# A new order for the head of a diffusion-transformer block: batch 0's roots on ScalarE, both of batch 0's K steps first, 2-byte statistics outputs

## The chip, the cores and the metric

One core of one Trainium2 chip. The metric is the device time of one execution in microseconds (us), as the median of several; executions of the kernel before spread from 243.1 to 244.75 us over all runs. "The profile" is one traced execution; its times count from the start of the span. PE is TensorE (PEld its weight loads), DVE VectorE, ACT ScalarE, POOL GpSimd, SP the engine that issues the loads.

## The reference, cut to what matters

```python
B, N, D = 2, 256, 1152            # bf16; F = 4 * D
mod = (_silu(c) @ w_mod).reshape(B, 6, 1, D)
shift_a, scale_a, gate_a, shift_m, scale_m, gate_m = [mod[:, i] for i in range(6)]
h = _layernorm(x, axis=-1) * (1 + scale_a) + shift_a
qkv = (h @ wqkv).reshape(B, N, 3, H, Dh)
...  # attention, wo, a second layernorm, fc1, gelu, fc2
```

The change touches only the way from `x` and `c` to the first matmuls of `K = h @ wk`. The 512 tokens lie in four tiles of 128: tiles 0 and 1 are batch 0, tiles 2 and 3 are batch 1. D is cut into 9 chunks of 128. The shift is added later; K needs `layernorm(x) * (1 + scale_a)`, transposed.

## The kernel before: the parts that matter

Statistics of tiles 1 and 3 are made on VectorE (`bn_stats`), those of tiles 0 and 2 on ScalarE, by two passes over 1152 elements whose outputs nobody reads; only the accumulated sums count.

```python
for t in (0, 1, 3, 2):                                   # order in which x lands
    nc.sync.dma_start(x_sb[:, t, :], x_v[:, t // TPB, t % TPB, :])
# then scale weights of chunks 0-1, K weights of 0 and 1, scale of 2-3, K of 2-3, scale of 4-5, ...
...
sink = act.tile([P, D], FP32, name="sink", tag="x1")
def act_stats(t):
    for f, dst in ((ACT.Identity, dsum), (ACT.Square, dsq)):
        nc.scalar.activation(sink[:], x_sb[:, t, :], f, bias=x_sb[:, t, 0:1], scale=-1.0,
                             accum_out=dst[:, t:t + 1])
def norm1(t, c0, c1):                                    # VectorE: (x - mean) * rstd
    ...
def scale_group(k0, k1, tile_of=aux_tile):               # PE: scale of chunks k0..k1 into pm
    ...
def modulate(pt, i, k, b, j0, eng):                      # hT0[k] of batch b = transposed xn * scale
    ...
def k_step(k, c0=0, c1=T, m0=0, m1=KM1):                 # chunk k of six K accumulators, tokens c0..c1
    for m in range(m0, m1):
        if k == 0 and c0 == 0:
            pk[m] = acc_tile([P, T], "pk")
        nc.tensor.matmul(pk[m][:, c0:c1], w_k[:, k, m * P:(m + 1) * P], hT0[:, k, c0:c1], ...)
...
warm(8, pwarm)                                           # matmuls on zeros while data comes
act_stats(0)
act_stats(2)
...
pool_rsqrt(0, 2)                                         # GpSimd: roots of tiles 0 and 1
...
norm1(1, 0, CUT)
norm1(0, 0, CUT)
pt_a = transpose_x([0, 1], BT[0])
...
pm0, pm1 = [scale_group(k, k + 1, acc_tile) for k in range(2)]
act_var(2)
nc.vector.tensor_scalar_mul(hT0[:, 0, 0:N], pt_a[:, 0, :], pm0[:, 0, 0:1])
...
transpose_x([0, 1], [3], pt_c, 1)
fill(1)                                                  # one more matmul on zeros
k_step(0, 0, N)                                          # batch 0, chunk 0
transpose_x([0, 1], [2], pt_c, 0)
k_step(1, 0, N)                                          # batch 0, chunk 1
modulate(pt_c, 0, 0, 1, 0, "d")
modulate(pt_c, 1, 1, 1, 0, "a")
...
k_step(0, N, T)                                          # batch 1, chunk 0
```

Every engine here runs its own instructions in program order (in c_before below VectorE idles 0.88 us in front of a variance, while batch 0's modulation stands behind it). "K step (k, b)" below is the six matmuls of chunk k for batch b.

## Time and profile before

243.88 us, median of 3 (243.38 to 244.41).

The page's busy time of PE, and the shares of the chain of waits:

```profile
PE 236.1 (98%) x1691; PEld 145.0 (60%) x1701; DVE 91.4 (38%) x193; ACT 59.8 (25%) x120; POOL 28.9 (12%) x48
...
PE 91%; DMA 3%; DVE 3%; ACT 1%; issue 1%; SPq 0%; POOL 0%; DVEq 0%; ACTq 0%
```

PE is the limit, so a change of the head can win only by letting PE's useful work begin earlier, or by closing gaps there. The timeline of PE in that stretch (start us, length us, engine, line, operation, out<-in, count, and in brackets idle time before it):

```profile
8.80 0.40 PE L264 MATMUL pt<-ident,xn 128*128 128x128 bf16 x4 [0.66 <-DVE xn L233]
9.13 0.17 PE L245 MATMUL pm<-ones_row 1*128 1x2 bf16 x1
9.24 0.60 PE L247 MATMUL pm<-sT,w_scale_a 128*128 128x2 bf16 x18
9.70 0.38 PE L323 MATMUL pwarm<-zeros 128*128 128x512 bf16 x1
9.92 0.27 PE L264 MATMUL pt<-ident,xn 128*128 128x128 bf16 x2
10.03 0.38 PE L323 MATMUL pwarm<-zeros 128*128 128x512 bf16 x1
10.24 0.82 PE L280 MATMUL pk<-big,w_k 128*128 128x256 bf16 x6
11.18 0.28 PE L264 MATMUL pt<-ident,xn 128*128 128x128 bf16 x2
11.30 1.49 PE L280 MATMUL pk<-big,w_k 128*128 128x256 bf16 x12
```

Read it so: batch 0's transposes at 8.80, the scale matmuls at 9.13, K step (0, batch 0) at 10.24, tile 2's transposes at 11.18, then twelve matmuls without a gap: K steps (1, batch 0) and (0, batch 1). The chain of waits there (start us, length us, what) passes through tile 2: its root on ScalarE, its normalisation, its transposes:

```profile
10.20 0.19 ACT rstd L229
10.39 0.02 issue
10.41 0.20 ACT rstd L230
...
10.71 0.43 DVE xn L233
11.13 0.05 issue
11.18 0.28 PE pt L264 x2
```

### The profile page before, as it was taken

How to read it: one execution, taken by the hardware profiler on the slowest of the kernel's cores; microseconds unless marked ns; L12 is line 12 of the kernel's file. 1: busy time of each engine (PE TensorE's matmuls, PEld its weight loads, DVE VectorE, ACT ScalarE, POOL GpSimd, SP SyncE). 2: the span in 40 equal slices, each digit the busy share in tenths (PEclk: the TensorE clock that was granted, in tenths of full speed). 3: DMA queues.
4: the chain of work that ended last, by engine and by line, in shares of the span. 5: the costliest groups of instructions: out<-in, count | busy, mean ns of one | idle time of the engine just before them, and what ended most of it. 6: DMA issues, size and time to landing. Idle time of an engine off the chain costs nothing.

```text
span 241.9 us, 3989 instructions
## 1 busy us (share of the span) xinstructions
PE 236.1 (98%) x1691; PEld 145.0 (60%) x1701; DVE 91.4 (38%) x193; ACT 59.8 (25%) x120; POOL 28.9 (12%) x48
## 2 busy tenths in 40 slices
PE   8899999999999999999999999999999999999994
PEld 5685444466667665888844444444656666566674
DVE  3742442319325678831002999960010000000001
ACT  6623322307215032671422333322000000000000
POOL 2400000002300324100000000001121111111111
PEclk9999999999999999999999999999999999999999
DMA  6999999996579999239999999999300000000000
GB/s 214 327 315 307 379 366 393 389 391 222 156 262 393 391 375 153 48 57 350 390 392 391 342 327 292 275 327 285 98 16 16 20 16 16 20 16 18 29 21 16
DMA packets 48781, 53.29 MB, mean 220 GB/s; under 512 B 9587, under 2 KB 36475, under 8 KB 48763
## 3 DMA queue, kind: packets, MB, share of 16 engines
q1 hardware_dynamic: 41312, 50.14, 62.4%
q10 hardware_dynamic: 6939, 1.71, 5.1%
q0 software_dynamic: 512, 1.19, 1.6%
q8 instruction: 13, 0.21, 0.4%
q14 instruction: 5, 0.04, 0.1%
HBM read 50.14 MB, written 1.19 MB: 212 GB/s over the span
## 4 chain that ended last, share of the span: by engine, by line
PE 91%; DMA 3%; DVE 3%; ACT 1%; issue 1%; SPq 0%; POOL 0%; DVEq 0%; ACTq 0%
PE pacc L790 29%; PE pacc L734 29%; PE pacc L590 7%; PE pq L512 7%; PE pk L280 5%; PE pacc L681 4%; PE pk L309 2%; PE pa L630 2%; PE ps_s L547 2%; DMA hT<-xn 2%; PE pn L407 2%; DMA x_sb<-in_x_dram 1%; DVE stats L193 1%; PE pt L264 1%; PE pm L247 1%
## 5 line engine op out<-in xcount | busy, mean ns | idle before, releaser
L734 PE MATMUL pacc<-hT,w_f 128*128 128x256 bf16 (+1 forms) x427 | 70.3, 325 | 0.4
L790 PE MATMUL pacc<-w_f,gT 128*128 128x384 bf16 (+2 forms) x468 | 70.5, 314 | 0.0
L790 PEld LDWEIGHTS <-gT 128*128 128x128 bf16 x468 | 44.4, 98 | 26.2
L734 PEld LDWEIGHTS <-w_f 128*128 128x128 bf16 x432 | 42.2, 98 | 27.9 <-issue 0.3
L796 DVE TENSOR_TENSOR tmp<-pacc,gate 128x384 f32<-128x384 f32 (+2 forms) x13 | 6.8, 527 | 65.6 <-PE pacc L790 57.2
L766 ACT ACTIVATE gT<-pacc 128x512 bf16<-128x512 f32 x24 | 14.3, 597 | 32.6 <-PE pacc L734 32.6
L460 DVE SCALAR_TENSOR_TENSOR part<-w_gate_m,s,part 128x1152 f32<-128x1152 bf16 x16 | 21.4, 1414 | 0.0
L798 POOL TENSOR_TENSOR o_sb<-tmp,x 128x384 bf16<-128x384 f32 (+1 forms) x12 | 11.7, 972 | 54.1 <-DVE tmp L796 54.1
L681 PE MATMUL pacc<-w_o,big 128*128 128x384 bf16 x108 | 17.9, 326 | 0.0
L512 PE MATMUL pq<-hT,w_q 128*128 128x512 bf16 x79 | 17.7, 379 | 0.1
L590 PE MATMUL pacc<-w_v,hT 128*128 128x384 bf16 x108 | 17.7, 326 | 0.0
L590 PEld LDWEIGHTS <-hT 128*128 128x128 bf16 x108 | 10.5, 98 | 7.1 <-issue 0.3
L681 PEld LDWEIGHTS <-big 128*128 128x128 bf16 x108 | 10.4, 98 | 7.2 <-issue 0.4
L512 PEld LDWEIGHTS <-w_q 128*128 128x128 bf16 x81 | 7.9, 98 | 9.4
L280 PE MATMUL pk<-big,w_k 128*128 128x256 bf16 (+1 forms) x70 | 12.9, 324 | 0.1
L687 POOL TENSOR_TENSOR x<-tmp,x_sb 128x384 f32<-128x384 f32 x8 | 7.3, 912 | 28.0 <-DVE tmp L686 28.0
L458 DVE TENSOR_SCALAR part<-w_gate_m,s 128x1152 f32<-128x1152 bf16 x2 | 1.5, 818 | 22.1 <-DMA w_gate_m<-in_w_mod_dram 22.1
L482 POOL DMA_DIRECT2D gates_dram<-nat_v x2 | 1.1, 534 | 67.4 <-DVE nat_v L480 67.4
L280 PEld LDWEIGHTS <-w_k 128*128 128x128 bf16 x72 | 6.7, 98 | 3.5
L755 ACT ACTIVATE gT<-pacc 128x512 bf16<-128x512 f32 x12 | 6.5, 598 | 8.9 <-PE pacc L734 8.9
L503 POOL DMA_DIRECT2D gates_dram<-nat x4 | 2.3, 584 | 49.4 <-DVE nat L500 48.8
L173 PE MATMUL pwarm<-zeros 128*128 128x256 f32 x20 | 6.9, 509 | 1.2 <-DVE eps_t L93 1.2
(101 smaller groups left out, 165.7 us busy)
## 6 DMA issues: line engine op xcount, KB each, us to landing
w_f<-in_w_fc_dram SPq DMA_DIRECT2D x12, 864.0 KB, 14.9
w_f<-in_w_fc_dram SPq DMA_DIRECT2D x3, 1728.0 KB, 7.8
w_f<-in_w_fc_dram SPq DMA_DIRECT2D x2, 2592.0 KB, 17.1
w_gate_a<-in_w_mod_dram SPq DMA_DIRECT2D x3, 864.0 KB, 12.3
w_v<-in_wqkv_dram SPq DMA_DIRECT2D x3, 864.0 KB, 13.8
w_o<-in_wo_dram SPq DMA_DIRECT2D x3, 864.0 KB, 14.0
w_shift_m<-in_w_mod_dram SPq DMA_DIRECT2D x3, 864.0 KB, 6.6
w_scale_m<-in_w_mod_dram SPq DMA_DIRECT2D x3, 864.0 KB, 13.0
```

Source lines behind the costliest of these rows:

```text
L173: nc.tensor.matmul(dst[:, 0:T // 2], zeros32[:, 0:P], zeros32, start=True, stop=True)
L280: nc.tensor.matmul(pk[m][:, c0:c1], w_k[:, k, m * P:(m + 1) * P], hT0[:, k, c0:c1], start=(k == 0 and c0 == 0), stop=(k == KD - 1), skip_g ...
L460: nc.vector.scalar_tensor_tensor(part[:, b, :], wg[:, k, :], s32[:, k, b:b + 1], part[:, b, :], op0=ALU.mult, op1=ALU.add,)
L512: nc.tensor.matmul(pq[m][:], w_q[:, k, m * P:(m + 1) * P], hT[:, k, :], start=(k == 0), stop=(k == KD - 1), skip_group_check=True,)
L590: nc.tensor.matmul(pacc[:], hT[:, k, t * P:(t + 1) * P], w_v[:, k, pnl * PW:(pnl + 1) * PW], start=(k == 0), stop=(k == KD - 1),)
L681: nc.tensor.matmul(pacc[:], aT[:, k, t * P:(t + 1) * P], w_o[:, k, c0:c1], start=(k == 0), stop=(k == KD - 1),)
L687: (nc.gpsimd if pool_add else nc.vector).tensor_tensor(x1[:, t, c0:c1], tmp[:], x_sb[:, t, c0:c1], op=ALU.add)
L734: nc.tensor.matmul(dst, w_f1[m // KD][:, k, ml * P:(ml + 1) * P], hT[:, k, c0:c1], start=start, stop=(k == KD - 1), **kw,)
L766: nc.scalar.activation(gT[:, m, :], pacc[:], ACT.Gelu_apprx_tanh)
L790: nc.tensor.matmul(pacc[:], gT[:, kk, t * P:(t + 1) * P], w_f2[j][:, r, c0 - n * PW:c0 - n * PW + cw], start=(kk == 0), stop=(kk == KF - 1),)
L796: nc.vector.tensor_tensor(tmp[:], pacc[:], gate_m[:, b, c0:c0 + cw], op=ALU.mult)
L798: (nc.vector if last else nc.gpsimd).tensor_tensor(o_sb[:], tmp[:], x1[:, t, c0:c0 + cw], op=ALU.add)
```

## The change

Intent: get batch 0's roots earlier (Ln and Exp on ScalarE in place of a power on GpSimd), do both of batch 0's K steps before anything of batch 1, make tile 2's root from its sums without a detour over VectorE, move two scale copies from ScalarE to VectorE, and let ScalarE's unused outputs go into the xn tiles as 2-byte elements. The diff, cut to its core:

```diff
-    sink = act.tile([P, D], FP32, name="sink", tag="x1")
-                sink[:], x_sb[:, t, :], f, bias=x_sb[:, t, 0:1], scale=-1.0,
+                xns[t][:], x_sb[:, t, :], f, bias=x_sb[:, t, 0:1], scale=-1.0,
...
+    def act_root(t):
+        nc.scalar.activation(rstd1[:, t:t + 1], dsq[:, t:t + 1], ACT.Ln, bias=dm2[:, t:t + 1], scale=1.0 / D)
+    def root_exp(t0, t1):
+        nc.scalar.activation(rstd1[:, t0:t1], rstd1[:, t0:t1], ACT.Exp, scale=-0.5)
+    def act_mean_eps(t):
+        act_sq_mean(t)
+        nc.gpsimd.tensor_scalar_add(dm2[:, t:t + 1], dm2[:, t:t + 1], LN_EPS)
+        act_mean(t)
-    warm(8, pwarm)
+    warm(7, pwarm)
     act_stats(0)
-    act_stats(2)
     for j in range(NPD):
         stats_piece(1, j)
...
-    act_var(0)
-    pool_rsqrt(0, 2)
+    act_mean_eps(0)
+    act_root(0)
+    nc.scalar.activation(rstd1[:, 1:2], mv1[:, 1, 1:2], ACT.Ln, bias=eps_t[:], scale=1.0)
+    root_exp(0, 2)
+    act_stats(2)
...
+    fill(1)                       # between batch 0's transposes and the scale matmuls
+    stats_piece(3, 2)             # the last third of tile 3 now behind norm1(1), norm1(0)
...
+    nc.vector.tensor_copy(scale_a[:, 0:1, :], pm0[:])
+    scale_add(pm1, 1, 2)
     modulate(pt_a, 1, 1, 0, 0, "d")
+    norm1(3, 0, CUT)
     norm1(2, 0, CUT)
     fill(1)
+    k_step(0, 0, N)
+    k_step(1, 0, N)
     pt_c = aux_tile([P, 2, N], "pt", BF16)
     transpose_x([0, 1], [3], pt_c, 1)
-    fill(1)
-    k_step(0, 0, N)
     transpose_x([0, 1], [2], pt_c, 0)
-    k_step(1, 0, N)
     modulate(pt_c, 0, 0, 1, 0, "d")
...
     for k in range(3, KD):
+        split = 2 if k == 5 else 0
+        k_step(k, 0, T, 0, split)  # two matmuls of K step 5 before the scale matmuls
...
-        k_step(k)
+        k_step(k, 0, T, split)
```

More of the change, by code (lines that the diff above doesn't have):

```diff
@@ L332, in pool_rsqrt @@
         )
-    warm(8, pwarm)
+    def act_root(t):
[7 more added lines that the diff above has]
+    warm(7, pwarm)
     act_stats(0)
-    act_stats(2)
     for j in range(NPD):
         stats_piece(1, j)
-    act_sq_mean(0)
-    nc.gpsimd.tensor_scalar_add(dm2[:, 0:1], dm2[:, 0:1], LN_EPS)
-    pool_eps(1)
+    act_mean_eps(0)
[3 more added lines that the diff above has]
+    act_stats(2)
     stats_piece(3, 0)
-    act_var(0)
-    pool_rsqrt(0, 2)
-    act_mean(0)
     stats_piece(3, 1)
+    norm1(1, 0, CUT)
+    norm1(0, 0, CUT)
+    pt_a = transpose_x([0, 1], BT[0])
+    fill(1)
     stats_piece(3, 2)
@@ L349 @@
     pool_rsqrt(3, 4)
-    norm1(1, 0, CUT)
-    norm1(0, 0, CUT)
-    pt_a = transpose_x([0, 1], BT[0])
-    act_sq_mean(2)
-    act_mean(2)
-    norm1(3, 0, CUT)
-    pm0, pm1 = [scale_group(k, k + 1, acc_tile) for k in range(2)]
-    act_var(2)
-    nc.vector.tensor_scalar_mul(hT0[:, 0, 0:N], pt_a[:, 0, :], pm0[:, 0, 0:1])
-    scale_add(pm1, 1, 2, "a")
-    modulate(pt_a, 1, 1, 0, 0, "d")
-    ln_exp_rsqrt(rstd1[:, 2:3], mv1[:, 2, 1:2])
-    nc.scalar.copy(scale_a[:, 0:1, :], pm0[:])
+    act_mean_eps(2)
+    act_root(2)
+    root_exp(2, 3)
+    pm0, pm1 = [scale_group(k, k + 1, acc_tile) for k in range(2)]
+    nc.vector.tensor_scalar_mul(hT0[:, 0, 0:N], pt_a[:, 0, :], pm0[:, 0, 0:1])
+    nc.vector.tensor_copy(scale_a[:, 0:1, :], pm0[:])
+    scale_add(pm1, 1, 2)
+    modulate(pt_a, 1, 1, 0, 0, "d")
+    norm1(3, 0, CUT)
     norm1(2, 0, CUT)
     fill(1)
+    k_step(0, 0, N)
+    k_step(1, 0, N)
     pt_c = aux_tile([P, 2, N], "pt", BF16)
     transpose_x([0, 1], [3], pt_c, 1)
-    fill(1)
-    k_step(0, 0, N)
     transpose_x([0, 1], [2], pt_c, 0)
-    k_step(1, 0, N)
     modulate(pt_c, 0, 0, 1, 0, "d")
```

## The prediction

> **What bounds the kernel now.** TensorE. The page gives PE 236.1 us busy of a 241.9 us span (98%); the chain of waits is 91% PE. From the first K matmul on (10.24 us in the timeline) PE has almost no gaps. The change touches only the first 25 us: it wins only by starting PE's real work earlier or closing gaps before 12 us; the rest is fixed PE work that shifts along.
>
> **The head before** (timeline, chain): x tile 1 lands 4.64; its statistics end on VectorE at 6.42; GpSimd's eps 6.54-6.77 and power 7.11-7.84; VectorE finishes tile 3's statistics (7.93-8.17), so the two normalisations run 8.08-8.75; transposes start at 8.80, modulated chunk 0 is ready 10.01, the first K step starts 10.24 behind two fill matmuls. Then tile 2's ScalarE statistics end at 9.42, its root 10.10-10.61, normalisation 10.71-11.12, its transposes start at 11.18 K step 1 covers the modulation, batch 1's K step 0 runs about 12.13-12.79.
>
> **The change, costed.**
> 1. Batch 0's roots move to ScalarE (Ln, Ln, one Exp; 0.28, 0.28, 0.20 in the trace, back-to-back ones overlapping by about 0.1). They wait for GpSimd's eps at 6.77: Ln about 6.80, Exp ends about 7.5, 0.34 before the old power result. VectorE has two of tile 3's pieces done by 7.4, so the normalisations run about 7.53-8.20 and the transposes start at about 8.25, 0.55 earlier.
> 2. First K step: weights for scale land at 8.62, K weights at 9.18: no wait. pm0 about 9.2, modulation to 9.58, first K step at about 9.6 against 10.24.
> 3. The price: tile 2's ScalarE statistics start about 7.45, not 6.68, and end about 10.16. GpSimd's tile 3 power comes first, so Ln starts about 10.2, Exp ends 10.7, normalisation about 10.75, transposes about 11.2: the same as before. Both batch 0 K steps are done by about 10.9, so PE idles about 0.25 before those transposes and about 0.55 after them, waiting for the modulation (about 11.58-11.93). Batch 1's K step 0 starts about 12.0 against 12.13. Net gain 0.1-0.15 us.
> 4. Two-byte outputs: nothing. The Trainium skill, "ScalarE: Activation LUTs" (What ACT_TABLE_LOAD costs), says one element per cycle for fp32 and bf16 alike, and about 93 ns per pointer operand. The trace agrees: 1.254 us with fp32 output and one pointer, 1.347 with bf16 output and two.
> 5. One warm-up less, scale copies on VectorE, K step 5 split: PE does not wait there; 0.
>
> **A ceiling.** Weights stream in order whatever compute does. The scale weights of chunks 4-5 land at 14.74 and are used at 15.49; no gain above 0.75 can pass.
>
> **Prediction.** 243.7 us, range 242.9 to 244.4. Faster by over 2%: 0.005; within 2%: 0.99; slower by over 2%: 0.005.
>
> **What would show it.** After: transposes at about 8.25; first K step at about 9.6; ScalarE's second square pass ending at about 10.2; two new waits in the list of waits, PE's weight load on tile 2's normalisation and PE on batch 1's modulation, together 0.6-0.9 us; the K steps with 512 columns starting within 0.2 us of 16.3; ScalarE's 1152-wide passes unchanged at 1.25 us.
>
> **What would make it wrong.** If tile 2's chain ends earlier than I say (shorter Ln/Exp, GpSimd faster), the gain grows to at most 0.7 us. If GpSimd's power for tile 3, now in front of tile 2's eps, is late, the gain vanishes or turns to a loss of 0.2. Scatter (243.38 to 244.41) exceeds the effect.

## The result, and the profile after

243.94 us, median of 4 (243.73 to 244.07), against 243.94 (243.38 to 244.41) of the kernel before, with one more run of it. Ratio 1.000, 95% interval 0.998 to 1.002: the same. A ratio here is the mean time of one kernel's runs over that of the other's of the same rounds, so not quite the ratio of the medians quoted.

The two lines of the page that answer to those of before:

```profile
PE 236.5 (98%) x1699; PEld 144.8 (60%) x1699; DVE 91.3 (38%) x193; ACT 59.9 (25%) x121; POOL 28.0 (12%) x47
...
PE 95%; DMA 3%; SPq 1%; DVE 0%; issue 0%; DVEq 0%
```

PE's timeline after the change:

```profile
8.20 0.38 PE L262 MATMUL pt<-ident,xn 128*128 128x128 bf16 x4 [0.23 <-DVE xn L231]
8.42 0.38 PE L321 MATMUL pwarm<-zeros 128*128 128x512 bf16 x1
8.73 0.17 PE L243 MATMUL pm<-ones_row 1*128 1x2 bf16 x1
9.10 0.60 PE L245 MATMUL pm<-sT,w_scale_a 128*128 128x2 bf16 x18 [0.19 <-DMA w_scale_a<-in_w_mod_dram]
9.56 0.38 PE L321 MATMUL pwarm<-zeros 128*128 128x512 bf16 x1
9.92 1.47 PE L278 MATMUL pk<-big,w_k 128*128 128x256 bf16 x12
11.23 0.39 PE L262 MATMUL pt<-ident,xn 128*128 128x128 bf16 x4
12.06 0.81 PE L278 MATMUL pk<-big,w_k 128*128 128x256 bf16 x6 [0.44 <-DVE big L268]
```

Batch 0's transposes came 0.60 us earlier (8.20 against 8.80), K step (0, batch 0) 0.32 earlier (9.92 against 10.24), and K step (0, batch 1) 0.08 later (12.06 against 11.98). The head start went into two waits of PE that this profile of the kernel before does not have: 0.19 for the scale weights (a second profile of it, c_before, has 0.45 there), and 0.44 for batch 1's modulation. The chain of waits no longer passes through tile 2's root, but through a load and PE's own order:

```profile
2.58 6.47 DMA w_scale_a<-in_w_mod_dram
9.05 0.05 issue
9.10 0.60 PE pm L245 x18
9.70 0.24 PE pwarm L321
9.94 1.45 PE pk L278 x12
11.39 0.24 PE pt L262 x4
11.63 0.03 issue
11.65 0.36 DVE big L268
```

What happens after K step (0, batch 1) is the same in both. From its start to the first Q matmul it took 20.20 us before and 20.24 after; from there to the first matmul of the output projection 45.24 and 45.25; the stretch up to the first fc1 matmul 20.27 and 19.99; from there to the end 144.17 and 144.18. So the span is the start of K step (0, batch 1), plus about 209.6 fixed, plus a stretch of about 20 that varies. This start is what the experiments look at, because it is sharper than the time: a gain of 0.3 us is 0.12%, and intervals are about 0.2% to each side.

One thing disturbs a comparison of single profiles. The first scale weights landed at 8.62 us in the profile before and at 9.05 after, tile 2 of x at 6.59 and 7.06, though nothing in the order of loads was changed.

### The profile page after: what moved, and what is told of

Its sections match the earlier page's. It is cut to its first block, busy times and chain, and to the rows that moved or that the text cites. A ratio compares the mean times of both kernels' runs of the same rounds, so it can differ in the third digit from the quotient of the medians. Undisturbed runs are those within 1.5% of the kernel's fastest.

```text
span 241.7 us, 3992 instructions
## 1 busy us (share of the span) xinstructions
PE 236.5 (98%) x1699; PEld 144.8 (60%) x1699; DVE 91.3 (38%) x193; ACT 59.9 (25%) x121; POOL 28.0 (12%) x47
## 4 chain that ended last, share of the span: by engine, by line
PE 95%; DMA 3%; SPq 1%; DVE 0%; issue 0%; DVEq 0%
PE pacc L742 29%; PE pacc L798 29%; PE pacc L689 7%; PE pacc L598 7%; PE pq L520 7%; PE pk L278 5%; DMA w_scale_a<-in_w_mod_dram 3%; PE pk L307 2%; PE pa L638 2%; PE ps_s L555 2%; PE pn L415 2%; PE pm L245 1%; PE pt L262 1%; SPq L86 1%; PE pg L497 0%
```

## The experiments

Theories named in the expectations. **T** is the prediction's: tile 2's chain (ScalarE's statistics, root, normalisation, transposes, modulation) sets batch 1's start, and moving ScalarE's work for tile 2 back eats the gain. **T2**: in the changed order PE's own program order sets it, counted from the landing of the scale weights. **W**: weights arriving in order limit the head whatever is done. **C**: the parts are each worth some tenths and cancel.

All starts, with the landings they hang on. K(0,0) and K(0,1) are the starts of chunk 0's K step for batch 0 and batch 1; "+" is counted from the landing of the first scale weights of the same profile.

| run | tile 2 of x lands | scale weights land | K(0,0) | K(0,1) | PE's wait before K(0,1) |
|---|---|---|---|---|---|
| before | 6.59 | 8.62 | +1.62 | 11.98, +3.36 | none |
| c_before | 7.65 | 9.63 | +1.34 | 12.59, +2.95 | none |
| e4_two_byte | 7.38 | 9.41 | +1.23 | 12.25, +2.84 | none |
| after | 7.06 | 9.05 | +0.87 | 12.06, +3.01 | 0.444 |
| c_after | 7.42 | 9.39 | +0.87 | 12.40, +3.01 | 0.443 |
| e6_tile2_free | 7.38 | 9.32 | +0.87 | 12.32, +3.01 | 0.443 |
| e5_no_split | 7.20 | 9.26 | +0.87 | 12.27, +3.01 | 0.442 |
| e2_pool_roots | 7.25 | 9.20 | +1.13 | 12.47, +3.27 | 0.441 |
| e1_k1_between | 7.72 | 9.67 | +0.87 | 12.49, +2.82 | none |
| e7_k1_halves | 7.05 | 9.14 | +0.87 | 11.91, +2.77 | 0.113 |
| b1_tile2_first | 7.59 | 9.56 | +0.87 | 12.26, +2.69 | 0.115 |
| b2_weights | 7.75 | 9.71 | +0.87 | 12.42, +2.71 | 0.114 |

The "+" is a latency from the landing only where PE waited for that landing. In before and e2 it did not: the scale matmuls stood behind late transposes (8.80 and 8.87), so these two would look smaller at a later landing.

(e3 loads these weights in two halves and stands apart.) Times: ratio to the kernel before, runs of each.

| run | median us | ratio, 95% interval | runs |
|---|---|---|---|
| c_before | 243.71 | 0.9999, 0.9975 to 1.0023 | 6 and 11 |
| e1_k1_between | 243.83 | 1.0001, 0.9982 to 1.0021 | 6 and 11 |
| e2_pool_roots | 244.20 | 1.0023, 1.0001 to 1.0044 | 6 and 11 |
| e3_scale_split | 244.17 | 1.0015, 0.9995 to 1.0034 | 6 and 11 |
| c_after | 244.24 | 1.0012, 0.9991 to 1.0033 | 6 and 11 |
| e6_tile2_free | 243.71 | 0.9993, 0.9976 to 1.0009 | 6 and 11 |
| e4_two_byte | 244.12 | 1.0009, 0.9985 to 1.0033 | 6 and 11 |
| b1_tile2_first | 243.85 | 0.9998, 0.9976 to 1.0021 | 6 and 11 |
| e7_k1_halves | 243.70 | 1.0004, 0.9992 to 1.0017 | 6 and 11 |
| b2_weights | 244.02 | 1.0019, 1.0006 to 1.0032 | 6 and 11 |
| e5_no_split | 243.77 | 1.0017, 1.0003 to 1.0032 | 4 and 11 |

Differences of 0.1 to 0.2% are not to be leaned on: c_before, the kernel before against itself, has an interval of 0.24% to each side.

### c_before: the kernel before against itself

No edit.

> Control: the kernel before against itself. All theories: ratio 1.000, and the interval's width says what a time can tell here (I expect about +-0.15%). Its profile shows how far the landings move by themselves: the first scale weights landed at 8.62 us in the profile before and at 9.05 after. If the change does not move them, this run lies anywhere between 8.6 and 9.1. If the change itself delayed them (rival), it lands at 8.6 again.

Measured: the scale weights landed at 9.63 us, 1.0 us later than in the first profile of the same program, and outside the 8.6 to 9.1 expected. So the landing moves by itself, and nothing shows that the change moved it. (The three later calls ran on three chips; within the last of them alone it was 9.14 to 9.71.) This profile also shows a dependence that the first one hid. Its chain of waits:

```profile
2.10 5.54 DMA x_sb<-in_x_dram
...
7.74 1.36 ACT sink L206 x2
9.10 0.02 issue
9.12 1.36 ACT sink L206 x2
10.47 0.02 issue
10.50 0.16 DVE mv L224
10.66 0.28 DVE big L358
```

In the kernel before, batch 0's first K step waits for tile 2, which belongs to batch 1: VectorE computes tile 2's variance (L224) in front of batch 0's modulation (L358), and keeps program order. With tile 2 landing late, at 7.65, that is the path. The changed kernel has no variance on VectorE; its K(0,0) comes 0.87 us after the scale weights in all six profiles with its head and one load of these weights, with tile 2 landing anywhere from 7.05 to 7.72. With its whole head the change brings K(0,0) forward by 0.36 to 0.75 us (+0.87 against +1.23 to +1.62), and this dependence is one part of that; how large a part was not tested alone. An estimate from the records of c_before: its first K step starts 0.51 us after the fill matmul in front of it (10.98 against 10.47), in the first profile 0.21, so about 0.3 there. The gain does not reach K(0,1).

### e1_k1_between: the order of before on PE

```diff
     k_step(0, 0, N)
-    k_step(1, 0, N)
     pt_c = aux_tile([P, 2, N], "pt", BF16)
     transpose_x([0, 1], [3], pt_c, 1)
     transpose_x([0, 1], [2], pt_c, 0)
+    k_step(1, 0, N)
```

> The changed kernel with batch 0's K step 1 put back between batch 1's transposes and its first K step, the order of before. Theory T (tile 2's chain and the uncovered modulation take the head start): the 0.44 us wait of PE for batch 1's modulation disappears, about 0.4 us of idle moves in front of the transposes of tiles 2 and 3, and batch 1's first K step starts 0.1 to 0.25 us earlier, at about 11.85 instead of 12.06; time within 0.1% of the changed kernel. Rival W (the arrival of weights limits everything): no start moves. Rival C (the parts of the change cancel, each worth some tenths): no statement on this one beyond that the time does not fall by the 0.44 us.

Measured: the 0.44 us wait is gone; of the 0.4 us of idle expected in front of the transposes, their starts show about 0.2 (tile 3's second at 11.45, tile 2's first at 11.71, where 0.06 is the usual distance). K(0,1) starts at +2.82 instead of +3.01, 0.19 earlier by the landing. The absolute 11.85 expected was not met (12.49), because the weights landed at 9.67; the expectation had counted from a fixed landing. The order on PE costs the changed kernel about 0.2 us. In this profile normalisation of tile 2 ended at 11.65 and its transposes started at 11.71, so here tile 2 is what limits: with the order put back, T's chain comes next. The time does not show 0.2 us.

### e2_pool_roots: batch 0's roots back on GpSimd

```diff
-    act_mean_eps(0)
-    act_root(0)
-    nc.scalar.activation(rstd1[:, 1:2], mv1[:, 1, 1:2], ACT.Ln, bias=eps_t[:], scale=1.0)
-    root_exp(0, 2)
+    act_sq_mean(0)
+    nc.gpsimd.tensor_scalar_add(dm2[:, 0:1], dm2[:, 0:1], LN_EPS)
+    pool_eps(1)
...
+    act_var(0)
+    pool_rsqrt(0, 2)
+    act_mean(0)
```

> The changed kernel with batch 0's two roots back on GpSimd and nothing else undone. Theory T: normalisations 0.4 to 0.55 us later (transposes at about 8.7), first K step at 10.1 instead of 9.92 because it also waits for weights that land near 9.05; the second square pass of tile 2 ends earlier, by what Ln and Exp took (at most 0.7 us, less if tile 2 lands late); batch 1's first K step at 12.1 to 12.3; time 0 to 0.2 us longer than the changed kernel. Rival C (the roots win about half a microsecond that another part gives back): 0.5 us longer than the changed kernel and than the kernel before.

Measured: transposes at 8.87, K(0,0) at +1.13 instead of +0.87, K(0,1) at +3.27 instead of +3.01. At this landing (9.20) the ScalarE roots are worth 0.26 us at K(0,1), less than the 0.6 to 0.7 that they bring to the transposes at best (8.20 against 8.80, 8.16 against 8.87): in the runs with them PE then waits for the scale weights. With a later landing they are worth less: b1 and b2 below have the roots on GpSimd, one fill matmul fewer in front of the scale matmuls, landings of 9.56 and 9.71, and +0.87 all the same. Both starts came later than T expected (10.33 for 10.1, 12.47 for 12.1 to 12.3), and 0.26 lies a little above its 0 to 0.2. The time can't tell T from C: a ratio of 1.0001 to 1.0044 to the kernel before holds both 0.2 and 0.5 us, and in this profile 0.42 us of the extra span lies far behind the head, in front of fc1 (20.41 against 19.99).

### e3_scale_split: the first scale weights in two loads

```diff
+        for a, z in [(0, 1), (1, 2)] if k0 == 0 else [(k0, k1)]:
-            w_scale_a[:, :, k0 * P:k1 * P],            # one load, then the K weights
+            w_scale_a[:, :, a * P:z * P],              # one load for each chunk, each with its K weights
```

> The changed kernel with the first scale weights loaded in two halves, chunk 0 alone first, each followed by its K weights: chunk 0's scale lands 0.5 to 0.9 us earlier. Rival W (weights limit): PE's 0.2 us wait for the scale weights goes, the first K step starts 0.3 us or more earlier, and batch 1's first K step and the whole time follow by the same 0.3 us. Theory T: the first K step starts earlier, but batch 1's first K step stays within 0.15 us of 12.06, since tile 2's normalisation ends at about 11.0 as before; no change of the time that can be seen.

A miss as a test. Chunk 0's weights landed at 8.09, but chunk 1's at 9.96, and PE multiplies both in front of K(0,0), so it waited 0.37 us for the second half and K(0,0) came at 10.46, K(0,1) at 12.60, far from T's 12.06. From K(0,0) to K(0,1) it is 2.14 with a wait of 0.443, the same as in the changed kernel. It says only that PE, with this order, needs both chunks. It showed something else. The normalisations ended at 8.02, but the transposes started at 8.63 without a wait; the warm-up matmuls were still running. (So too in e5, e6 and e7: transposes at 8.56, 8.38 and 8.42, normalisations done by 8.02.) The timelines of e3 and, second, of e2:

```profile
3.30 5.49 PE L173 MATMUL pwarm<-zeros 128*128 128x256 f32 x14
8.63 0.39 PE L262 MATMUL pt<-ident,xn 128*128 128x128 bf16 x4
```

```profile
3.30 4.00 PE L173 MATMUL pwarm<-zeros 128*128 128x256 f32 x14
```

The same fourteen matmuls took 5.49 us and 4.00. By their records they start 427 ns apart at first and 216 ns apart later, and the step between the two fell at 7.73 us in e3 and at 4.74 in e2. The Trainium skill, "TensorE: Matmul & The Clock Gate" (Part 1), tells of such a cold phase, half as fast, and that it is "run-variable"; the trace agrees.

### c_after: the changed kernel again

No edit.

> The changed kernel again, beside the others of this call. From the six profiles so far the first scale weights land anywhere from 8.62 to 9.67 us and tile 2 of x from 6.59 to 7.72, in unchanged programs too. Theory T2 (in the changed kernel batch 1's first K step comes a fixed 3.0 us after the scale weights land: scale matmuls, modulation, two K steps, four transposes, one uncovered modulation): it starts at landing + 2.9 to 3.1 us, with the same 0.44 us wait in front. Time ratio to before 0.998 to 1.002.

Measured: K(0,1) at +3.01 with a wait of 0.443, as in the first profile to 0.01 us, though the scale weights landed 0.34 us later and tile 2 of x 0.37. T2's constant holds. It is made of: 0.87 to K(0,0), 1.31 for two K steps (9.92 to 11.23 in the first profile), and 0.83 from the first transpose to K(0,1). The 0.83 is a latency nothing covers: four transposes, VectorE's modulation of 0.35, and handing over. The Trainium skill (same page, "Single matmul latency") gives (398 + N) / 2.4 ns for one matmul, an estimate of 219 ns for the last transpose from start to result; the records have 219. The ends of matmuls in a profile are modelled, so that alone proves little; but VectorE started on the result 0.25 us after the last transpose's start (11.65 against 11.40), which leaves no room for much more.

### e6_tile2_free: tile 2 without its own statistics

```diff
     def norm1(t, c0, c1):
+        s = 3 if t == 2 else t
-            xns[t][:, c0:c1], x_sb[:, t, c0:c1], mv1[:, t, 0:1], rstd1[:, t:t + 1],
+            xns[t][:, c0:c1], x_sb[:, t, c0:c1], mv1[:, s, 0:1], rstd1[:, s:s + 1],
...
-    act_stats(2)
-    act_mean_eps(2)
-    act_root(2)
-    root_exp(2, 3)
```

> The changed kernel with tile 2 freed of its own statistics and root: it takes tile 3's instead, ScalarE's two passes, Ln and Exp for it are gone. The result is wrong on purpose. Theory T (tile 2's statistics chain on ScalarE limits batch 1, as the prediction said): PE's 0.44 us wait for batch 1's modulation shrinks or goes and batch 1's first K step starts 0.3 us or more earlier after the scale weights' landing. Theory T2 (the order on PE limits: transposes come only after both K steps, then nothing covers the modulation): the wait stays at 0.4 to 0.45 us and batch 1's first K step still starts 2.9 to 3.1 us after that landing; time equal to the changed kernel's.

The result was wrong on purpose (relative error 0.07). PE's timeline up to 12.8 us, and VectorE's line of the normalisations of tiles 3 and 2:

```profile
10.19 1.47 PE L279 MATMUL pk<-big,w_k 128*128 128x256 bf16 x12
11.49 0.39 PE L263 MATMUL pt<-ident,xn 128*128 128x128 bf16 x4
12.32 0.71 PE L279 MATMUL pk<-big,w_k 128*128 128x256 bf16 x5 [0.44 <-DVE big L269]
```

```profile
10.57 0.73 DVE L232 TENSOR_SCALAR xn<-x_sb,mv,rstd 128x512 bf16<-128x512 bf16 x2
```

With 2.5 us of ScalarE passes and the root of tile 2 gone, the wait is 0.443 and K(0,1) at +3.01: nothing moved. ScalarE's chain for tile 2 is not the limit of the changed kernel; T falls there. A caution: the normalisation of tile 2 did not end earlier either (11.29, 1.98 after the weights, as in the profile after), since VectorE does it behind the scale copies, batch 0's modulation and tile 3's normalisation. It ends 0.2 us before the transposes start, so VectorE is the next in line, not the limit. So e6 acquits ScalarE's part alone; the run that separates PE's order from the normalisation is e7.

### e4_two_byte: 2-byte outputs alone, on the kernel before

```diff
-    sink = act.tile([P, D], FP32, name="sink", tag="x1")
-                sink[:], x_sb[:, t, :], ...
+                xns[t][:], x_sb[:, t, :], ...
```

> The kernel before with ScalarE's statistics outputs as 2-byte elements in the xn tiles, and nothing else of the change. All theories but C: ScalarE's four passes stay at 1.25 us each, ratio to before 0.999 to 1.001. Rival C (a part that wins is hidden by one that loses): passes of 1.1 us or less and 0.3 us faster.

ScalarE's statistics passes by the view of one line (duration in ns, min/median/max), first the kernel before, then e4:

```profile
L206 ACT ACTIVATE sink<-x_sb x4: 1254/1256/1256, 3.6 to 8.1; 128x1152 f32<-128x1152 bf16 x4
```

```profile
L204 ACT ACTIVATE xn<-x_sb x4: 1254/1254/1255, 3.7 to 8.8; 128x1152 bf16<-128x1152 bf16 x4
```

No difference in the passes and none that can be told in the time. The output's width is nothing here, as the Trainium skill ("ScalarE: Activation LUTs") says: one element per cycle for fp32 and bf16 alike.

### b1_tile2_first: a try at a better version

Roots of batch 0 on GpSimd as before, tile 2's statistics when it lands and its root in the new form, no fill before the scale matmuls, and K step (1, batch 0) in two halves around batch 1's transposes:

```diff
     act_stats(0)
+    act_stats(2)
...
-    act_root(0)
-    root_exp(0, 2)
+    act_var(0)
+    pool_rsqrt(0, 2)
...
+    norm1(3, 0, CUT)                 # before batch 0's modulation
...
     k_step(0, 0, N)
-    k_step(1, 0, N)
+    k_step(1, 0, N, 0, 3)
     transpose_x([0, 1], [3], pt_c, 1)
     transpose_x([0, 1], [2], pt_c, 0)
+    k_step(1, 0, N, 3)
```

> A try at a version that beats both: roots of batch 0 on GpSimd as before, so that ScalarE starts tile 2 when it lands; tile 2's root in the new form, right after its statistics; scale copies on VectorE; no fill in front of the scale matmuls; batch 0's K step 1 split around batch 1's transposes, three matmuls before and three after. Theory T2: no wait over 0.1 us is left in front of batch 1's modulation, its first K step starts 0.3 to 0.5 us earlier than in before or after at the same landings (scale weights' landing + 2.5 to 2.7 us); time 0.1 to 0.2% shorter, at the edge of what can be told. Rival W (weights in order, the scale weights of chunks 4 and 5 above all): PE gets those 0.3 to 0.5 us back as a wait for those weights, and the time does not fall.

Measured: K(0,1) at +2.69, 0.32 earlier than the changed kernel and 0.15 to 0.26 earlier than the order of before at like landings (+2.84 and +2.95), the latter short of the 0.3 to 0.5 expected; a wait of 0.115 is left, a little over the 0.1 expected. The scale weights of chunks 4 and 5 landed at 15.76 and were taken at 15.81, so the next limit was one step away (W in its narrow form). From K(0,1) to the first Q matmul it took 20.29 us, 0.05 more than the 20.24 of after, e7 and b2, so at most that much was given back. The ratio is 0.9998: a head that is 0.15 to 0.26 us better than that of the kernel before is not seen in the time.

### e7_k1_halves: only the cover, nothing else

```diff
     k_step(0, 0, N)
-    k_step(1, 0, N)
+    k_step(1, 0, N, 0, 3)
     pt_c = aux_tile([P, 2, N], "pt", BF16)
     transpose_x([0, 1], [3], pt_c, 1)
     transpose_x([0, 1], [2], pt_c, 0)
+    k_step(1, 0, N, 3)
```

> The changed kernel with one thing moved: three of the six matmuls of batch 0's K step 1 go behind batch 1's transposes, to cover the modulation. Theory T2 (PE order): PE's 0.44 us wait falls under 0.2 us, and batch 1's first K step starts 2.65 to 2.8 us after the scale weights land, not 3.0. If tile 2's normalisation limits all the same (theory T), it stays at 2.9 us or more. The time: 0.1% shorter than the changed kernel at most, inside the interval.

PE's timeline:

```profile
10.02 1.14 PE L278 MATMUL pk<-big,w_k 128*128 128x256 bf16 x9
10.99 0.47 PE L262 MATMUL pt<-ident,xn 128*128 128x128 bf16 x4
11.30 1.42 PE L278 MATMUL pk<-big,w_k 128*128 128x256 bf16 x9
```

Three matmuls moved behind the transposes: the wait falls from 0.44 to 0.113, K(0,1) from +3.01 to +2.77. That is T2's forecast (2.65 to 2.8), by an edit that touches no statistics and no root, while tile 2's normalisation ended as ever (11.12, 1.98 after the weights). It can't give much more: tile 2's transposes started at 11.18, 0.08 behind PE's usual pace, so tile 2 is the limit from here. (The nine matmuls at 11.30 are the three of K step (1, batch 0) and, from 11.91, the six of K(0,1).)

### b2_weights: the try, with one K weight load moved

```diff
-        for a, z in [(0, 1), (1, 2)] if k0 == 0 else [(k0, k1)]:
+        for a, z in {0: [(0, 1), (1, 2)], 2: [(2, 3)], 4: [(3, 4), (4, 6)]}.get(k0, [(k0, k1)]):
```

> The try at a better version with the K weights of chunk 3 loaded behind the scale weights of chunks 4 and 5 instead of in front of them, so that these land about 0.55 us earlier. Rival W in its narrow form (in the earlier try PE reached those scale weights 0.05 us after they landed, so they had become the next limit): they now land 0.4 us or more before PE takes them, no new wait appears, and batch 1's first K step still starts 2.6 to 2.75 us after the first scale weights. Time 0.1 to 0.2% under before if the head were all; but eight profiles so far scatter by 0.7 us in the span for other reasons, so I expect an interval that holds 1.

The scale weights of chunks 4 and 5 landed at 15.38 and were taken at 15.94: 0.56 us of room instead of 0.05, and K(0,1) at +2.71. The head did what was asked. The time is 0.19% longer, not shorter, with an interval that leaves out 1. In its profile PE waited late, at 98.7 us, for the second layer norm. The wait, and the load of the chain in front of it:

```profile
PE pacc L744 <- DVE hT L663: 0.7, 1, 0.7
```

```profile
93.95 4.35 DMA hT<-xn
```

The same transposing load took 3.74 us in the first profile before, 3.88 in e2 and 4.03 in c_after, where PE waited 0.12, 0.26 and 0.40; in the eight profiles without a wait whose traces tell its landing it took 3.24 to 3.32. From the first matmul of the output projection to the first of fc1 it took 19.98 or 19.99 us in nine of the thirteen profiles, and 20.27 in before, 20.41 in e2, 20.55 in c_after and 20.81 in b2. So the stretch of about 20 that varies follows this load; why it takes longer in some executions the profiles do not say. I know of no link from the moved load to that place, and did not test one; whether b2 is really slower stays open. It is not a version that beats both.

### e5_no_split: K step 5 whole

```diff
-        split = 2 if k == 5 else 0
+        split = 0
```

> The changed kernel with K step 5 whole again. All theories: PE does not wait there in any profile so far (scale weights of chunks 6 to 8 land 0.8 us or more before they are used), so no time; the stretch from K step 4 to K step 6 is 0 to 0.05 us shorter. Rival W in its strong form would show a wait for those scale weights.

K(0,1) at +3.01 as in the changed kernel, no wait for the scale weights of chunks 6 and 7 (they landed at 18.50 and were taken at 19.27, a room of 0.77, a little under the 0.8 expected). From K(0,1) to the first Q matmul it took 20.20 us against 20.24, so the split costs 0.04 and guards against nothing that any profile shows.

## Why the prediction was right

The number was right: 243.94 us, 0.24 over the 243.7 forecast, inside 242.9 to 244.4. That says little about the mechanism: the range is 1.5 us wide, some ten times the forecast gain, and a small gain, none or a small loss would all have fallen in it. The mechanism was right in outline: a head start for batch 0 that batch 1's first K step gives back, through an uncovered modulation. Point by point:

- **Roots on ScalarE, transposes at about 8.25.** Ln began at 6.57 and the transposes at 8.20. Right, with help: tile 1 landed 0.23 us earlier than in the profile before.
- **First K step at about 9.6.** It came at 9.92. The mis-sized term is the landing of the scale weights, taken as fixed at 8.62. It was 9.05, and over the profiles it is 8.62 to 9.71. Counted from the landing the step is +0.87. But an earlier landing would have helped only as far as PE waited for it: in this profile the scale matmuls could have started about 0.26 earlier (0.10 after the matmul at 8.73, as in the kernel before, instead of at 9.10), so at a landing of 8.62 I estimate 9.66.
- **Tile 2's chain, "the same as before", as the price.** Its times were nearly right (second square pass ending at 9.90 for 10.16, normalisation ending at 11.03 for about 11.16, the 10.75 forecast and the 0.41 that it takes). Its role was wrong in every profile of the changed kernel. With the first K step 0.32 later than forecast, both K steps ended about 0.3 later too, at 11.2, and filled the 0.25 of idle in which PE was to wait for tile 2. e6 took ScalarE's part of it away and nothing moved; e7 left all of it and moved three matmuls and K(0,1) came 0.24 us earlier. The give-back comes from putting both K steps in front of the transposes. So the first of the two waits forecast, PE's weight load on tile 2's normalisation, did not appear: together they were 0.44 and not 0.6 to 0.9.
- **Net gain 0.1 to 0.15 us.** K(0,1) was 0.08 us later, with weights that landed 0.43 later. At like landings it is a small loss too: e4, which has the order of before, and c_after (weights at 9.41 and 9.39, tile 2 at 7.38 and 7.42) have 12.25 and 12.40. That 12.06 is so near the forecast 12.0 is partly luck: it was reached through late weights and PE's order, not through tile 2. Of the 0.21 us between forecast (12.0 against 12.13) and measurement (12.06 against 11.98), 0.15 is a misreading: I took 12.13 for the start in the kernel before from the chain of waits, where pieces begin when the piece before them ends; the instruction's own record says 11.98.
- **2-byte outputs nothing, split nothing.** Right: 1254 to 1256 ns either way; 0.04 us.
- **A ceiling of 0.75 us from the scale weights of chunks 4 and 5.** Right in kind. It moves with the landings; in b1 the room had shrunk to 0.05 us.

What stays open: whether the changed kernel wins when the weights land as early as 8.62 us. K(0,1) came at 11.98 in the kernel before. The constant +3.01 would give 11.63, but it holds only while PE waits for the weights; with the 0.26 us of above I estimate 11.80, and tile 2, whose normalisation ended no earlier than 11.03 in any profile with the changed head, could make it later. No such profile had so early a landing.

## What to carry to other kernels

When work is moved forward on the bounding engine, look at what it used to cover: the K step that stood between the transposes and their use was hiding 0.4 us of latency, and moving it in front exposed that. Count starts from the landing that they hang on, as long as they do hang on it, and not from time zero, and take a second profile of the unchanged kernel before explaining differences of some tenths. An engine in program order can hang one batch's work on another's data, as the variance of tile 2 did in front of batch 0's modulation; a late load brings it out.

## What the Trainium skill lacked or had wrong

- "DMA: Bandwidth & Descriptors" has nothing on how far the landing of the same first loads moves from run to run. With the loads up to there unchanged, twelve profiles had the first scale weights landing between 8.62 and 9.71 us and tile 2 of x between 6.59 and 7.75. K(0,1) starts anywhere between 11.91 and 12.59 in them, more than any edit here moved it.
- "TensorE: Matmul & The Clock Gate", Part 1, says the transition out of the cold phase varies by ±500 ns. Here the step from 427 to 216 ns between warm-up matmuls fell between 4.74 and 7.73 us, a range of 3.0, with the first matmul at 1.18 each time. The profile's view gives a granted clock of 1.00 for the first 5 us all the same: the clock records of the trace begin only near the step (at 7.79 us in e3, 4.76 in e2), and what lies in front of them counts as full. So the spacing is the thing to read.
- The same page, Part 4, gives about 275 ns for a 128x128 bf16 transpose in a kernel. The records of the first stage here have 216 to 230 ns from start to end and mostly 55 to 67 between starts, near the page's own single-matmul formula (219). The ends are modelled, but VectorE took the result of the last one 0.25 us after its start.
- No page warns that a transposing load in the chain varies enough (3.24 to 4.35 us here) to stall PE for 0.12 to 0.66 us in some executions and not in others.
